# Layer two of a sixth batch in seven half-size products, scores in 64x32 tiles, and a new order of all pieces

## The chip, the cores and the metric

The kernel runs on one core of a Trainium2 chip. The metric is the device time of one execution in microseconds (us), the median of several runs. PE is TensorE (PEld its weight loads), DVE is VectorE, ACT is ScalarE, POOL is GpSimd, SP is SyncE, which here only issues DMAs.

## The reference

Eight batches, each with 8 heads of 512 tokens by 64 channels (`x`) and 32 states by 64 channels (`state`). Cross attention goes both ways, and the result, 544 rows by 512 channels for each batch, goes through a two-layer network:

```python
scores  = scale * x @ state.T;  a  = softmax(scores)     # per head, over 32 states
xread   = a @ state
scores2 = scale * state @ x.T;  a2 = softmax(scores2)    # per head, over 512 tokens
sread   = a2 @ x
X = concat([xread, sread], axis=2)                       # then heads side by side: (8*544, 512)
h = X @ w_in                                             # 512 -> 2048
g = s * relu(h)**2 + b
out = g @ w_out                                          # 2048 -> 512
```

## The kernel before

**An order written out by hand.** The whole kernel is a list of words, `ORDER`. Each word calls one small function (`pieces`), which issues its instructions; every engine executes its instructions in the order of the words. A word is a name and its arguments: `M.3.0.0` is batch 3, columns 0 to 511 of w_in; a last letter A, V or G names the engine (ACT, DVE, POOL). `idle.12` issues twelve matmuls on ones, whose result nobody uses (tile `dps`).

**Attention.** For a batch, `x` loads the tokens as half floats (`xh`), `xT` turns them in 32x32 blocks on DVE, and `T` computes the scores on PE: for each of two channel halves `e`, four head places `hp` and two head groups `g`, one matmul of a 32x32 tile, so 16 for a batch, with states from `stE`, which `pair` makes by a block transpose of the states `stn`. Group g writes half g of the tile T. `keep` copies scores to SBUF. Then, for the first softmax, U (transpose), mu (max), D (subtract), E1 (exp), z (sum and reciprocal), At (scale) and A (transpose). The second softmax is nm, nms, E2, a2; `aps` and `a2T` transpose it, `V` multiplies it with the tokens in another layout (`xn`), and `srd` keeps the result for the rows of all states, which go through the network at the end (`lsr`, `ssr`, `S_sr`, `P_sr`, `ev_sr`). In batch 0, x, xT, T and the first softmax come in two halves (a last argument 0 or 1), and part of its tokens come through `xf` and `castx`.

**Layer one.** Since xread = a @ state, the kernel first multiplies states and w_in: `M` is eight matmuls in 64x32 tiles (tile `mps`), and `Mc` copies the result to SBUF as half floats. Then `l.b.f` is two matmuls of 512 columns for one of 16 feature blocks (tile `hps`) and a relu on ACT; `s` squares two or four of them into the tile `g`. `lh` and `sh` are the same for half of batch 0's tokens.

**Layer two, direct.** `L.b.rr.q` is four matmuls of 512 columns; four of them make a token block of 128 rows, which `out` scales, shifts (on DVE) and stores. Sixteen L for a batch.

**Layer two, in seven products.** For batches 3 to 7 tokens, features and output channels are each split in two, and the eight half-size products become seven, with sums of halves: `S` makes sums of g on DVE or POOL (S1, S2, S4 in place, S3 in a tile of its own), `wsum` makes T1 to T4 from w_out once, `P.b.u` (u from 0 to 13) is eight steps of 256 columns times two row blocks, half of one product, `ev` takes a finished product out of PSUM on DVE, and `put` stores. The banks X, Y and W share two PSUM buffers with the direct products. A product that goes into X again waits until the one before has been evicted:

```python
PRODUCTS = [
    ("X", (0, 0), (0, 0)), ("Y", (0, 1), (1, 0)), ("X", (0, 0), "T2"), ("W", (1, 0), "T1"),
    ("X", None, "T3"), ("W", (0, 1), (1, 1)), ("X", (1, 1), "T4"),
]
```

The output tiles `osx_0` and `osx_1` exist once each, so that a batch's first eviction waits for the stores of the batch before.

**Queues.** POOL issues the loads of weights, tokens and states (`win`, `wout`, `x`, `xn`, `st`) in one queue with its own arithmetic; SP issues nearly all stores.

Of the kernel before, what the change touches and what calls it, by code (L numbers as in the profile page):

```python
# [10 lines left out]
FP32 = mybir.dt.float32  # L11
FP16 = mybir.dt.float16
# [66 lines left out]
def kernel(  # L79
# [12 lines left out]
    nc = tc.nc  # L92
    AF = mybir.ActivationFunctionType
    ALU = mybir.AluOpType
    AX = mybir.AxisListType

    B, H, S, D = x.shape
    Ns = state.shape[2]
    DM = H * D
    DF = moe_w_in.shape[1]  # L100
    P = 128
    NK = DM // P
    NKF = DF // P
    NG = H // 4
# [3 lines left out]
    NR = B * H * Ns // P  # L108
# [51 lines left out]
    stE = konst.tile([P, NR, Ns, 2], FP16, name="stE")  # L160
# [60 lines left out]
    nc.vector.memset(ones32, 1.0)  # L221
    xh_t[0] = xpool.tile([P, NG, NT, D], FP16, name="xh_0", tag="xh")
# [32 lines left out]
    def pair_states(i0, i1):  # L255
        nc.vector.transpose(
            stE[:, i0:i1].rearrange("p i n e -> p (i n e)").bitcast(FP32),
            stn[:, i0:i1].rearrange("p i d -> p (i d)").bitcast(FP32),
        )

# [33 lines left out]
    def at_T(b, own=1, p=None):  # L294

        at[b]["T", p] = T = two_banks(f"T_{b}_{p}", own=own)
        for e in range(2):
            for hp in range(4):
                for g in range(NG):
                    r = hp ^ g  # L300
                    mm(
                        part(T[Ns * hp : Ns * hp + Ns], p, g)[:, 0, :],
                        stE[32 * r : 32 * r + 32, NG * b + g, :, e],
                        part(at[b]["xT"][32 * r : 32 * r + 32, :, :, e], p, g)[:, 0, :],
                        start=(e == 0), stop=(e == 1),
                        tp=(32 * r, Ns * hp),
                    )
# [450 lines left out]
```

## Time and profile before

| | |
|---|---|
| time, median of 3 runs | 218.65 us (218.47 to 218.85) |
| the profiled execution | 218.68 us, span 216.8 us |
| granted PE clock, mean | 0.998 |
| busy: PE, DVE, ACT, POOL | 95%, 78%, 71%, 48% of the span |
| DMA | 103 GB/s on average, 153 to 205 GB/s in the first 32 us |

The page gives busy times by engine, the granted clock, and the chain of work that ended last. In the timeline a row is a group of instructions with its start, its time, the engine, the line and the tiles (out<-in), and in brackets the engine's idle time before it with what ended it. A row of windows is a stretch, its length, and the busy time of PE, PEld, DVE, ACT and POOL, each with its count, then the clock, the DMA share and GB/s. Matmuls overlap: the time of one in the trace is longer than the distance to the next.

### The profile page before, as it was taken

Reading aid. Unit: us, or ns where it says so; the run is one execution under the profiler, and the core shown is the slowest. Engines: PE = TensorE matmul, PEld = TensorE weight load, DVE = VectorE, ACT = ScalarE, POOL = GpSimd, SP = SyncE. Lnnn points to the kernel's source line nnn. Section 1 sums busy time; section 2 is a strip of 40 time slices with the busy share of each in tenths; the row PEclk is TensorE's granted clock in tenths of the full one; section 3 lists DMA queues with packets and bytes.
Section 4 is the critical chain, followed back from the end, with each engine's and each line's share of the span. In section 5 each row is a group of like instructions: output and inputs, shape, how many; then the busy total and the mean of one; then the engine's idle time right before and its main releaser. Section 6 shows DMA issues by size and latency. Waiting matters only on the chain.

```text
span 216.8 us, 4729 instructions
## 1 busy us (share of the span) xinstructions
PE 207.0 (95%) x1920; PEld 126.4 (58%) x1920; DVE 169.4 (78%) x236; ACT 154.7 (71%) x262; POOL 105.0 (48%) x102
## 2 busy tenths in 40 slices
PE   7668999999999999999999999999999999999992
PEld 2334444344444434545677666776667777888881
DVE  2699885989867879986998799979887964785571
ACT  4378987898858788899889899667668866444400
POOL 8529123494679930525254318836564334225330
PEclk9999999999999999999999999999999999999999
DMA  6999992759497262192908850718903600450055
GB/s 153 186 205 205 199 197 42 125 124 133 106 173 120 48 99 49 38 155 55 144 9 137 139 110 4 97 39 139 205 10 65 131 0 3 87 111 0 0 153 141
DMA packets 23657, 22.42 MB, mean 103 GB/s; under 512 B 4436, under 2 KB 17492, under 8 KB 23636
## 3 DMA queue, kind: packets, MB, share of 16 engines
q0 software_dynamic: 16848, 12.52, 40.8%
q1 hardware_dynamic: 5504, 8.66, 16.4%
q10 hardware_dynamic: 1284, 0.95, 1.6%
q8 instruction: 15, 0.25, 0.5%
q14 instruction: 6, 0.05, 0.1%
HBM read 25.72 MB, written 8.91 MB: 160 GB/s over the span
## 4 chain that ended last, share of the span: by engine, by line
PE 90%; ACT 5%; DMA 2%; DVE 0%; issue 0%; SPq 0%
PE hps L461 24%; PE ops L505 19%; PE opf_X L137 16%; PE opf_W L137 8%; PE mps L137 4%; PE opf_Y L137 4%; PE hps_sr L461 3%; PE vps L137 2%; DMA xf<-in_x_dram 2%; ACT M L152 2%; PE aps L137 2%; PE ops_sr_X L137 2%; PE T_None L137 2%; ACT rh L491 1%; PE dps L672 1%; PE hph L137 1%
## 5 line engine op out<-in xcount | busy, mean ns | idle before, releaser
L465 ACT ACTIVATE r<-hps 128x512 f16<-128x512 f32 x120 | 67.5, 602 | 27.8 <-PE hps L461 26.3
L461 PE MATMUL hps<-A,M 128*128 128x512 f16 x240 | 64.7, 380 | 0.0
L137 PEld LDWEIGHTS <-g 128*128 128x128 f16 x480 | 46.6, 98 | 11.4 <-issue 0.7
L505 PE MATMUL ops<-w_out,g 128*128 128x512 f16 x192 | 46.3, 379 | 0.0
L471 POOL TENSOR_TENSOR g<-r 128x1024 f16<-128x1024 f16 (+1 forms) x14 | 30.4, 2180 | 23.7 <-ACT r L465 23.7
L461 PEld LDWEIGHTS <-M 128*128 128x128 f16 x240 | 21.7, 98 | 22.7 <-issue 6.2
L505 PEld LDWEIGHTS <-g 128*128 128x128 f16 x192 | 18.7, 98 | 22.2 <-issue 0.4
L152 ACT CAST M<-mps 128x1024 f16<-128x1024 f32 x22 | 22.3, 1017 | 1.6 <-PE mps L137 1.5
L469 ACT ACTIVATE g<-r 128x1024 f16<-128x1024 f16 (+1 forms) x18 | 21.4, 1210 | 0.1
L192 POOL DMA_DIRECT2D xn<-in_x_dram x32 | 18.6, 592 | 5.6 <-PE vps L137 4.9
L346 POOL TENSOR_TENSOR At<-E,rz 128x1024 f16<-128x1024 f16 x5 | 9.8, 1964 | 22.0 <-ACT r L465 11.3
L137 PE MATMUL opf_X<-w_T,g 128*128 128x256 f16 x160 | 19.8, 272 | 0.0
L575 DVE TENSOR_TENSOR g<-g 128x1024 f16<-128x1024 f16 (+1 forms) x20 | 17.9, 908 | 1.1 <-POOL S L575 0.9
L575 POOL TENSOR_TENSOR g<-g 128x1024 f16<-128x1024 f16 x4 | 8.8, 2207 | 19.6 <-PE opf_X L137 12.4
L471 DVE TENSOR_TENSOR g<-r 128x1024 f16<-128x1024 f16 (+1 forms) x18 | 14.7, 836 | 1.6 <-ACT r L465 1.6
L152 DVE CAST M<-mps 128x1024 f16<-128x1024 f32 x10 | 12.1, 1213 | 3.5 <-PE mps L137 3.0
L604 DVE SCALAR_TENSOR_TENSOR osx<-opf_X,sb_bc,bias_bc 128x512 f32<-128x512 f32 x15 | 11.2, 746 | 4.0 <-PE opf_X L137 3.9
L292 DVE STREAM_TRANSPOSE xT<-xh 128x1024 f32<-128x1024 f32 (+2 forms) x12 | 10.4, 869 | 4.7 <-ACT xh L152 4.1
L325 POOL TENSOR_TENSOR Dm<-U,mu 128x1024 f32<-128x1024 f32 x3 | 5.7, 1913 | 15.0 <-DVE mu L321 15.0
L465 ACT ACTIVATE r_sr<-hps_sr 128x256 f16<-128x256 f32 x16 | 6.1, 382 | 7.9 <-PE hps_sr L461 7.2
L137 PE MATMUL mps<-w_in,stT 64*32 64x512 f16 x256 | 11.2, 383 | 0.3
L515 DVE SCALAR_TENSOR_TENSOR osb<-ops,sb_bc,bias_bc 128x512 f32<-128x512 f32 x12 | 8.8, 737 | 3.4 <-PE ops L505 3.4
(101 smaller groups left out, 324.3 us busy)
## 6 DMA issues: line engine op xcount, KB each, us to landing
out_dram<-osx SPq DMA_DIRECT2D x36, 128.0 KB, 2.4
xn<-in_x_dram POOLq DMA_DIRECT2D x32, 128.0 KB, 5.1
xh<-in_x_dram POOLq DMA_DIRECT2D x14, 256.0 KB, 5.1
w_in<-in_moe_w_in_dram POOLq DMA_DIRECT2D x8, 256.0 KB, 8.3
w_out<-in_moe_w_out_dram POOLq DMA_DIRECT2D x4, 512.0 KB, 11.2
out_dram<-osb SPq DMA_DIRECT2D x16, 128.0 KB, 2.6
out_dram<-osb SPq DMA_DIRECT2D x16, 64.0 KB, 4.4
xf<-in_x_dram SPq DMA_DIRECT2D x2, 256.0 KB, 3.7
```

The lines of the kernel that those rows point to most:

```text
L137: return nc.tensor.matmul(out, lhsT, rhs, start=start, stop=stop, tile_position=tp, is_transpose=is_transpose, skip_group_check=skip,)
L152: (engine.copy if engine is nc.scalar else engine.tensor_copy)(out, in_)
L192: nc.gpsimd.dma_start(out=xn_t[b][32 * jh : 32 * jh + 32].rearrange("t h c d -> t h (c d)"), in_=x[b].rearrange("h (t jh c) d -> jh t h (c ...
L292: nc.vector.transpose(part(out, p, g), part(in_, p, g))
L346: e.tensor_tensor(out, E1, over_n(rz), ALU.mult)
L461: nc.tensor.matmul(hps, lhsT, rhs, start=(i == 0), stop=(i == len(terms) - 1))
L465: nc.scalar.activation(R_t[tag, q][:, i], hps, AF.Relu)
L469: nc.scalar.activation(g, r, AF.Square)
L471: e.tensor_mul(g, r, r)
L505: nc.tensor.matmul(ops_t[tag, rr], G_t[tag][:, f, P * rr : P * rr + P], w_out_f(f), start=(f == 0), stop=(f == NKF - 1),)
L575: e.tensor_tensor(out, x, y, op)
L604: nc.vector.scalar_tensor_tensor(out, fast(b, name[0]), s_bc, out if plus else bias, ALU.mult, ALU.add)
```

## The change

1. Batch 2's layer two is done in seven products, as in batches 3 to 7: 16 words L and 4 words out go; 14 P, 8 half sums S, 7 ev and 4 put come (P 70 to 84, ev 35 to 42, put 20 to 24), and the sums of w_out are made earlier, eight half ones on DVE.
2. `T` uses 64x32 tiles, the size that `M` uses. Two states share the 64 rows of a tile, so the states are stored twice, `stZ[0]` and `stZ[1]`, each with the other's rows zero: `pair` transposes, then scales by a column of ones and zeros (`own`) twice. Heads are placed by `hp ^ 2 * g` instead of `hp ^ g`.
3. The words stand in a new order with other engines: squares on ACT, DVE, POOL from 18, 18, 14 to 11, 30, 9; M's casts on ACT and DVE from 22, 10 to 29, 3; V in six words instead of four; idle from 12, 12 and 5 to 7, 5 and 4. Only the beginning of the list is shown.

```diff
 ORDER = [
-    "x0.1 x0.0 castx.1.A xT.0.1.0 casts.A idle.12 pair.0.4 castx.0.A xT.0.0.0 T.0.1.0 U.0.0 turn.0.4.A "
-    "mu.0.0 D.0.V.0 E1.0.0 sb idle.12 keep.0.0 xT.0.1.1 win.0 M.1.0.0 M.0.0.1 x.1 z.0.0 xT.0.0.1 At.0.V.0 "
-    "A.0.0 win.1 wout.0 T.0.0.1 U.0.1 Mc.1.0.A mu.0.1 D.0.V.1 Mc.0.0.A lh.0.2.0 xT.1.1 lh.0.0.0 keep.0.1 "
-    "xT.1.0 idle.5 E1.0.1 win.2 M.0.1.0 T.1.1 sh.0.0.0.V Mc.0.1.A z.0.1 At.0.V.1 A.0.1 lh.0.6.0 lh.0.4.0 "
...
+    "casts.A pair.0.4 castx.1.A idle.7 xT.0.1.0 castx.0.A xT.0.0.0 x0.1 xT.0.1.1 x0.0 idle.5 turn.0.4.A "
+    "T.0.1.0 U.0.0 win.0 win.1 keep.0.0 x.1 win.2 wout.0 xT.0.0.1 T.0.0.1 mu.0.0 D.0.V.0 win.3 keep.0.1 "
+    "U.0.1 M.1.0.1 M.0.0.0 E1.0.0 Mc.1.0.A z.0.0 mu.0.1 D.0.V.1 At.0.V.0 A.0.0 wout.1 Mc.0.0.A E1.0.1 "
+    "idle.4 st z.0.1 At.0.V.1 M.0.1.1 Mc.0.1.A M.1.1.0 Mc.1.1.A xT.1.0 A.0.1 x.2 lh.0.2.0 sh.0.2.0.V "
+    "lh.0.0.0 sh.0.0.0.V lh.0.6.0 sh.0.6.0.V lh.0.2.1 xT.1.1 sh.0.2.1.V wout.2 sb lh.0.4.1 M.0.2.0 "
...
-    stE = konst.tile([P, NR, Ns, 2], FP16, name="stE")
+    stZ = [konst.tile([P, NR, Ns, 2], FP16, name=f"stZ_{k}") for k in range(2)]
+    own = konst.tile([P, 2], FP32, name="own")
...
+    nc.vector.memset(own, 0.0)
+    for r in range(4):
+        nc.vector.memset(own[Ns * r : Ns * r + Ns, r % 2 : r % 2 + 1], 1.0)
...
         nc.vector.transpose(
-            stE[:, i0:i1].rearrange("p i n e -> p (i n e)").bitcast(FP32),
+            stZ[0][:, i0:i1].rearrange("p i n e -> p (i n e)").bitcast(FP32),
             stn[:, i0:i1].rearrange("p i d -> p (i d)").bitcast(FP32),
         )
+        for k in (1, 0):
+            nc.vector.tensor_scalar(stZ[k][:, i0:i1], stZ[0][:, i0:i1], own[:, k : k + 1], None, ALU.mult)
...
-                    r = hp ^ g
+                    r = hp ^ 2 * g
+                    rows = slice(64 * (r // 2), 64 * (r // 2) + 64)
                     mm(
                         part(T[Ns * hp : Ns * hp + Ns], p, g)[:, 0, :],
-                        stE[32 * r : 32 * r + 32, NG * b + g, :, e],
-                        part(at[b]["xT"][32 * r : 32 * r + 32, :, :, e], p, g)[:, 0, :],
+                        stZ[r % 2][rows, NG * b + g, :, e],
+                        part(at[b]["xT"][rows, :, :, e], p, g)[:, 0, :],
                         start=(e == 0), stop=(e == 1),
-                        tp=(32 * r, Ns * hp),
+                        tp=(64 * (r // 2), Ns * hp),
                     )
```

The part of the new order that the middle of batch 4's seven products comes from:

```
... M.6.0.1 a2.6 s.4.12.4.V S.4.3.0.V S.4.3.1.V M.5.3.0 ev.3.X4
l.5.0 Mc.6.0.A put.2.1.0 put.2.1.1 put.3.0.0 l.5.6 P.4.2 P.4.3 x.7 S.4.1.2.V z.6 At.6.V l.5.3 P.4.0
S.4.2.0.G xT.7 Mc.5.3.A P.4.1 ev.4.X1 ev.4.Y l.5.4 l.5.1 aps.6 a2T.6.A S.4.2.1.V s.5.0.2.V l.5.9
P.4.4 P.4.5 l.5.5 T.7.1 M.6.2.0 put.3.0.1 keep.7 A.6 ev.4.X2 ...
```

More of the change, by code (lines that the diff above doesn't have):

```diff
@@ L410, in at_V @@
                 for g in range(NG):
-                    hp = k ^ g
+                    hp = k ^ 2 * g
                     for i in range(SCH):
@@ L430, in at_M @@
             for g in range(NG):
-                r = hp ^ g
+                r = hp ^ 2 * g
                 mm(
```

113 rows, old and new, of the table ORDER are left out of this document.

## The prediction

> **What bounds the kernel now.** I read the page's busy shares, the chain of waits, PE's own waits, then PE's timeline.
>
> ```profile
> PE 207.0 (95%) x1920; PEld 126.4 (58%) x1920; DVE 169.4 (78%) x236; ACT 154.7 (71%) x262; POOL 105.0 (48%) x102
> PE 90%; ACT 5%; DMA 2%; DVE 0%; issue 0%; SPq 0%
> ```
>
> PE is busy 95% of the span and is 90% of the chain that ends last. Its waits (us in total, times, longest) lie in the first 22 us:
>
> ```profile
> PE T L137 <- DVE xT L292: 1.3, 1, 1.3
> PE T L137 <- ACT M L152: 0.9, 1, 0.9
> PE hph L137 <- ACT M L152: 0.7, 2, 0.5
> PE hph L137 <- ACT rh L491: 0.3, 1, 0.3
> ```
>
> After that matmuls start one behind the other, so what counts is the distance from start to start, not the duration of one. PE's timeline (start, us, engine, line):
>
> ```profile
> 27.04 1.89 PE L505 MATMUL ops<-w_out,g 128*128 128x512 f16 x8
> 28.77 0.59 PE L461 MATMUL hps<-A,M 128*128 128x512 f16 x2
> ...
> 48.80 0.59 PE L461 MATMUL hps<-A,M 128*128 128x512 f16 x2
> 49.33 0.64 PE L137 MATMUL T_None<-xT,stE 32*32 32x512 f16 x16
> 49.90 0.41 PE L137 MATMUL mps<-w_in,stT 64*32 64x512 f16 x8
> 50.25 1.04 PE L461 MATMUL hps<-A,M 128*128 128x512 f16 x4
> ...
> 164.14 1.91 PE L137 MATMUL opf_X<-w_T,g 128*128 128x256 f16 x16
> 165.89 1.03 PE L461 MATMUL hps<-A,M 128*128 128x512 f16 x4
> ```
>
> Eight full matmuls take 28.77 - 27.04 = 1.73 us (0.216 each), sixteen half-size ones 165.89 - 164.14 = 1.75 us (0.109 each). Words of ORDER thus cost PE: L 0.863, P 0.873, l 0.432, lh 0.436. Added up so, the words behind L.0.1.1 (ended 28.77) come to 183.4 us; PE ended 212.49, so the remaining 0.3 us is all the waiting in 184 us.
>
> **Product form.** Batch 2 loses 16 L (16 x 0.863 = 13.81) and gains 14 P (14 x 0.873 = 12.22): **-1.60 us** on the path.
>
> **Tiles.** A T costs 0.57 (49.33 to 49.90) and the M behind it 0.35; two M in a row take 0.56 in all. I read this as 0.22 per eight matmuls, 0.12 at the end of each stretch of one tile size, and 0.10 on entering. Before there are 23 entries and 29 stretches, after 26 and 26, since T and M now share a size: 3 x 0.10 - 3 x 0.12 = about -0.1 us. Bounds: T as before (+0.3), or one entry fewer for each pair (-0.5).
>
> **V.** Six words instead of four; a pair costs 1.14 and an entry 0.10, so +0.2 us (up to +1.1 if a single V cost as much as a pair). Dense work: -1.60 - 0.1 + 0.2 = **-1.5 us**.
>
> **The start** I follow instruction by instruction from rows. The first T still waits for the second half of xf (cast at 5.63, transposed by 6.73), so it stays at 6.78: the five small memsets and two scalings in front of it end earlier. No row shows a scaling of this shape; the nearest (L388, 128x512) is 0.363, the memset of 128x512 0.485. I take 0.2 each for the first pair and 0.5 for the second (384 columns before, scaled as 768), with zero and twice that as ends. DVE now does U, mu and D of both halves before the first z chain ends, so A.0.0 ends near 13.8 (12.7 before); ACT casts four M before the first relu, which begins near 15.7 (13.99 before). On POOL nothing but DMA issues stands before sh.0.4.0, while in before w_in 3 was issued behind a square that waited for ACT to 14.67. Landings in before are some 2.45 us per weight load from 10.6 (w_in 0) to 23.8 (w_in 3); in the new order that puts w_in 1 at 13, w_in 2 at 18.0 (21.2 before), w_out 0 at 20.5 (17.9 before), w_out 1 at 25.5, w_out 2 near 32. With relus of 0.55 from 15.7 and these landings L.0.1.1 ends at 29.3, with 14.6 us of useful PE work done (14.2 at 28.77 before): **+0.1 us**. Bounds: -0.5 (relus start earlier) to +1.0 (a landing late). The fillers (29 dps before, 16 now) only fill gaps.
>
> **The rest.** ACT's work by rows goes from 174.2 to 176.1, POOL's from 106.0 to 87.4, DVE's from 178.8 to 191.4 (out 12 to 8, ev 35 to 42, S 26 to 41, s 18 to 30, Mc 10 to 3) plus 1.4 for the scalings. For these PE is the cover, where DVE keeps up:
>
> ```profile
> 100.00:150.00 50.00, 50.00 (x557) 35.06 (x556) 44.17 (x64) 41.94 (x70) 26.07 (x27) 1.00 0.56 90
> ```
>
> DVE is busy 44.2 of 50 us here (fifth column). In this stretch rows give 46.5 us of DVE words before and 50.5 after, so 48 of 50 us are to be expected. Following DVE's queue from ev.2.X4 to ev.4.W2, I find every result ready before PE needs it, but barely: S.4.2.1 0.1 us before P.4.5, ev.4.X1 0.5 before P.4.4; at P.2.7 S.2.1.1 comes 0.1 late. One wait is new: batch 3's ev.3.X1 writes the single osx_0 that batch 2 now uses, and z, At, xT and the sums of batches 3 to 6 queue behind it on DVE. Batch 2's last eviction into it ends near 92.7, its four stores (2.4 us to landing, some 0.5 us apart on SP) are out by 97, ev.3.X1 is due at 98.3; were it late, P.3.4 at 104.4 would be the first to feel it. Batch 2's stores stay eight of 128 KB. I allow 0.7 us of waits where before has 0.3: **+0.4 us**, bounds 0 and +2.5. The end is unchanged: seven small products, one eviction of 0.48 and a store.
>
> Sum: -1.5 + 0.1 + 0.4 = **-1.0 us**. The profiled execution took 218.68 (span 216.8), the median is 218.65; so **217.7 us**.
>
> **Rivals.**
>
> *DVE comes too late* (slower). Each product into bank X waits until the one before is evicted, and evictions stand in DVE's queue behind z, At, xT and sums. From S.3.2.0 to ev.4.Y thirty instructions hold about 24.5 us and run from 102.8 to 128.3 with 0.5 us to spare. If DVE needs over 2% more than my rows, P.4.4 waits; at 6% it is 1.5 us less the 0.5, and about 1 us again in the next 20 us, since PE has no slack to make it up. With -1.1 from the other terms: near **219.6**. For it: one-half sums take 0.69 to 0.78 us by shape, and 2.04 at 194.15, while POOL worked too. Against: POOL has 18.6 us less to do, and before holds 88% without a wait.
>
> *A slow PE clock in the start* (about no change). The granted clock reads 1.00 everywhere, yet the first fillers start 0.43 apart:
>
> ```profile
> 1.46 4.05 PE L672 MATMUL dps<-ones 128*128 128x512 f16 x12 [1.46 <-DVE ones L220]
> ...
> 8.19 2.76 PE L672 MATMUL dps<-ones 128*128 128x512 f16 x12
> ```
>
> The second twelve run at 0.22. In the changed kernel both first groups run out near 5.5, and until M at 10.7 PE has only two T, two transposes and the like, 1.3 us of work in 5.2. If it falls back to half speed there, four M, the four fillers and the first two lh take twice their 1.1, 0.9 and 0.9 us; part lies beside ACT's casts, so it costs 0.6 to 1.2, and the result is **218.6**. The Trainium skill, "TensorE: Matmul & The Clock Gate", Part 1, says that the array's clock halves after an idle window of about 3.4 us and returns after a busy one; the first twelve fillers agree, while a stretch as thin as this one is shown by no run here. By that rule the slow stretch would be likely, by the row at 8.19 (full speed after 2.7 thin us) not.
>
> *The wider tile is slower.* If products of two row positions into one half of T took turns, a T would go from 0.57 to about 1.0 and seven full and two half ones would cost +3.4: **221**. Against: in before four row positions write into each half, and T costs what M costs, where each half has one row position. The Trainium skill, "TensorEngine Tiling (Array Packing)", Gotcha 1, says that different row tiles cannot use one PSUM bank at once; the 0.57 against 0.56 speaks against a cost.
>
> *The start gains* (faster): w_in 2 lands 3 us sooner, and if relus keep pace L.0.1.1 ends at 28.6 and waits stay at 0.3: **216.5**.
>
> **How the numbers follow.** Chances: forecast 0.49, DVE late 0.24, slow clock 0.12, wider tile 0.04, start gains 0.11. A measurement here tells 0.2% (0.44 us). The forecast's own range is 216.7 to 218.5. Faster: most of the forecast (0.44), the start that gains and little of the clock: 0.58. Same: 0.05 of the forecast, 0.07 of the clock and some of DVE late: 0.15. Slower: the rest, 0.27. The range leaves out the wider tile and the worst of DVE: 216.1 to 219.9.
>
> **What would show it.** Right: L.0.1.1 ends near 29.3, from there to PE's end some 182.2 us, P of batch 2 at 0.873, a T in front of an M at 0.44 to 0.46, DVE at 95% in the 100 to 150 window. Wrong: PE waiting for osx, g or S on DVE in the middle; lh or M at twice their distance before 20 us; T near 1 us.

## The result and the profile after

| | before | after |
|---|---|---|
| median of 20 runs each, same chip | 218.76 us (218.24 to 219.44) | 218.13 us (217.52 to 218.81) |
| ratio after to before, 95% interval | | 0.9967 [0.9957, 0.9978] |
| profiled execution (span) | 218.68 us (216.8) | 217.52 us (215.7) |
| L.0.1.1 ends | 28.77 | 29.13 |
| last product starts | 211.62 | 210.59 |
| between the two | 182.85 | 181.46 |

The kernel is faster by 0.72 us by the ratio (0.0033 of 218.76; interval 0.48 to 0.94); the two medians differ by 0.63. The forecast was 1.0 us and 217.7; the measured median lies inside its own range. The profiled execution of the changed kernel is the fastest of its twenty, so its distance from before (1.16 us) is more than the usual one. The last row of the table is used throughout: "the body" is the time from L.0.1.1's end to the start of the last product. The two orders do not put the same work ahead of it: in the changed kernel PE has done two `l` and the four transposes of turn.4.12 more by then and one `lh` less, 0.65 us by rows.

The page, busy shares and the chain that ended last:

```profile
PE 205.8 (95%) x1955; PEld 130.0 (60%) x1955; DVE 179.6 (83%) x277; ACT 158.0 (73%) x260; POOL 86.9 (40%) x94
PE 91%; DMA 3%; ACT 2%; POOL 1%; DVE 1%; issue 0%; POOLq 0%
```

PE is still the chain. DVE went from 78% to 83% of the span, POOL from 48% to 40%. PE's waits (us in total, times, longest):

```profile
PE T L141 <- DVE xT L302: 1.8, 2, 1.2
PE dps L683 <- DVE ones L225: 1.5, 1, 1.5
PE mps L141 <- DMA w_in<-in_moe_w_in_dram: 1.3, 2, 0.9
PE hph L141 <- ACT rh L502: 0.7, 1, 0.7
PE mps L141 <- DVE M L156: 0.4, 1, 0.4
```

All of these lie before 26 us; behind that the profile shows no wait of PE at all. PE's timeline (start, us) at the two places that the prediction named:

```profile
58.99 0.65 PE L141 MATMUL T_None<-xT,stZ 64*32 64x512 f16 x16
59.46 0.40 PE L141 MATMUL mps<-w_in,stT 64*32 64x512 f16 x8
59.79 0.61 PE L472 MATMUL hps<-A,M 128*128 128x512 f16 x2
...
82.43 1.91 PE L141 MATMUL opf_Y<-w_out,g 128*128 128x256 f16 x16
84.17 1.04 PE L141 MATMUL opf_X<-w_T,g 128*128 128x256 f16 x8
85.05 0.59 PE L472 MATMUL hps<-A,M 128*128 128x512 f16 x2
```

T in front of M takes 59.46 - 58.99 = 0.47 (before 0.57), and T and M together 0.80 where before they took 0.92. Two P of batch 2 take 84.17 - 82.43 = 1.74 and one takes 0.88, as P of the other batches did before (one P is eight matmuls: four steps of 256 columns times two row blocks). The stage from 100 to 150 us (PE, PEld, DVE, ACT, POOL busy, then PE's clock):

```profile
100.00:150.00 50.00, 50.00 (x574) 35.42 (x575) 47.57 (x73) 43.33 (x71) 20.11 (x25) 1.00 0.53 91
```

DVE is busy 47.6 of 50 us (48 forecast, 44.2 before), and PE is full.

### The profile page after: what moved, and what is told of

It reads as the page before. It is cut to its first block, busy times and chain, and to the rows that moved or that the text cites. A ratio compares the mean times of both kernels' runs of the same rounds, so it can differ in the third digit from the quotient of the medians.

```text
span 215.7 us, 4829 instructions
## 1 busy us (share of the span) xinstructions
PE 205.8 (95%) x1955; PEld 130.0 (60%) x1955; DVE 179.6 (83%) x277; ACT 158.0 (73%) x260; POOL 86.9 (40%) x94
## 4 chain that ended last, share of the span: by engine, by line
PE 91%; DMA 3%; ACT 2%; POOL 1%; DVE 1%; issue 0%; POOLq 0%
PE hps L472 25%; PE opf_X L141 20%; PE ops L516 13%; PE opf_W L141 10%; PE opf_Y L141 5%; PE mps L141 5%; DMA w_in<-in_moe_w_in_dram 3%; PE hps_sr L472 3%; PE vps L141 2%; PE aps L141 2%; PE ops_sr_X L141 2%; PE T_None L141 2%; ACT M L156 1%; PE hph L141 1%; PE ops_sr_W L141 1%; PE dps L683 1%
## 5 line engine op out<-in xcount | busy, mean ns | idle before, releaser
L482 POOL TENSOR_TENSOR g<-r 128x1024 f16<-128x1024 f16 (+1 forms) x9 | 21.3, 2372 | 27.0 <-ACT r L476 22.8
L156 ACT CAST M<-mps 128x1024 f16<-128x1024 f32 x29 | 29.2, 1013 | 2.3 <-PE mps L141 1.9
L516 PE MATMUL ops<-w_out,g 128*128 128x512 f16 x128 | 30.7, 379 | 0.0
L482 DVE TENSOR_TENSOR g<-r 128x1024 f16<-128x1024 f16 (+1 forms) x30 | 22.1, 754 | 1.6 <-ACT r L476 1.6
L586 POOL TENSOR_TENSOR g<-g 128x1024 f16<-128x1024 f16 (+1 forms) x3 | 8.3, 2768 | 15.4 <-PE opf_X L141 8.1
L141 PE MATMUL opf_W<-w_out,g 128*128 128x256 f16 x96 | 12.4, 273 | 0.0
L141 PE MATMUL opf_W<-w_T,g 128*128 128x256 f16 x96 | 12.3, 273 | 0.0
L141 PE MATMUL opf_X<-w_out,g 128*128 128x256 f16 x96 | 12.1, 273 | 0.0
L141 PE MATMUL opf_X<-w_T,S 128*128 128x256 f16 x96 | 11.8, 273 | 0.0
L141 PE MATMUL opf_Y<-w_out,g 128*128 128x256 f16 x96 | 11.8, 273 | 0.0
```

Of the source, the lines that this page charges most:

```text
L141: return nc.tensor.matmul(out, lhsT, rhs, start=start, stop=stop, tile_position=tp, is_transpose=is_transpose, skip_group_check=skip,)
L156: (engine.copy if engine is nc.scalar else engine.tensor_copy)(out, in_)
L482: e.tensor_mul(g, r, r)
L516: nc.tensor.matmul(ops_t[tag, rr], G_t[tag][:, f, P * rr : P * rr + P], w_out_f(f), start=(f == 0), stop=(f == NKF - 1),)
L586: e.tensor_tensor(out, x, y, op)
```

## The experiments

Each kernel was timed beside the kernel before on the same chip; ratios are to that, with 95% intervals. The changed kernel's own is 0.9967.

### Product form: direct, direct2, pe8

**direct** puts batch 2 back to the direct form:

```
-P.2.0 ... P.2.1 ... P.2.13            (fourteen P, with S.2.*, ev.2.*, put.2.*)
+L.2.0.0 ... L.2.0.3 out.2.0 ... L.2.3.2 L.2.3.3 out.2.3   (sixteen L, at the places of the P)
```

> The changed kernel with batch 2's layer two direct: sixteen L and four out in the places of its fourteen P, no S, ev or put for batch 2. My theory: PE pays the product form's 1.60 us back and nothing else changes: 218.04 + 1.6 = 219.6, ratio to before 1.004; DVE has some 8 us less to do and that is worth nothing. Rival, DVE's load is what costs in the changed kernel: part of the 1.6 comes back and the ratio is 0.998 to 1.001.

Measured: 223.74 us, ratio 1.0244 [1.022, 1.0268], some 6 us above the changed kernel. Compared start by start with the changed kernel, PE is 0.45 later at L.0.1.1 and 2.07 later at the `l` that starts at 96.15 there (l.4.2): 1.62 us have come on. Fourteen L stand there against twelve P, 1.60 by the rows, and the last two of each cost the same, so this is the product form, neither more nor less. What follows is another thing. PE at 104 us, and DVE at the same time:

```profile
104.93 1.03 PE L466 MATMUL hps<-A,M 128*128 128x512 f16 x4
107.84 0.65 PE L135 MATMUL T_None<-xT,stZ 64*32 64x512 f16 x16 [1.88 <-DVE xT L296]
```

```profile
105.13 0.75 DVE L520 SCALAR_TENSOR_TENSOR osb<-ops,sb_bc,bias_bc 128x512 f32<-128x512 f32 x1 [3.98 <-PE ops L510]
105.80 0.74 DVE L609 SCALAR_TENSOR_TENSOR osx<-opf_X,sb_bc,bias_bc 128x512 f32<-128x512 f32 x1
106.46 1.24 DVE L296 STREAM_TRANSPOSE xT<-xh 128x1024 f32<-128x1024 f32 x1
```

The eviction out.2.3 stood at the head of DVE's queue for 3.98 us, waiting for L.2.3.3, and xT.6 stood behind it, so that T.6.1 came 1.9 us late. A second wait (0.9 us at 156, P.5.4) makes up most of the rest, and it is of another kind: ev.5.X1, which P.5.4 needs, writes osx_0, and batch 4's last store out of osx_0 landed at 155.07 by the trace, 5.2 us after its issue, so that the eviction started at 155.25. In the changed kernel that store landed at 148.30, 2.4 us after its issue, and the same eviction started at 149.38. By these times it is the wait for the single osx_0 that the prediction named, at another batch; why the store took longer is open. So the surplus came from the places that I gave to the words and from that store, not from PE's work.

**direct2** moves the last two L and their eviction forward:

```
-L.2.3.0 L.2.3.1 l.4.2 ... l.4.5 L.2.3.2 L.2.3.3 out.2.3
+L.2.3.0 L.2.3.1 L.2.3.2 L.2.3.3 out.2.3 l.4.2 ... l.4.5
```

> The changed kernel with the sixteen L and four out of batch 2 in place of its fourteen P, sums and evictions, as in the run before it (direct), but with L.2.3.2, L.2.3.3 and out.2.3 right behind L.2.3.1, so that the last eviction of batch 2 no longer holds up ev.3.X1 and xT.6 in DVE's queue. Product form is worth 1.6 us (direct's trace shows PE 1.62 later at the end of batch 2, and the other 3 us as waits behind that eviction): 1.6 to 2.2 us more than the changed kernel, ratio to before 1.004 to 1.007, and no wait of PE at T.6.1. Rival, that products in the direct form cost more than their rows or leave DVE too late in any place: 3 us or more over the changed kernel, ratio above 1.010.

Measured: 223.41 us, 1.0197 [1.0162, 1.0233]; the rival's figure, not mine. The wait did not go, it changed its owner:

```profile
105.87 1.08 PE L466 MATMUL hps<-A,M 128*128 128x512 f16 x4 [0.85 <-ACT r L470]
107.27 0.65 PE L135 MATMUL T_None<-xT,stZ 64*32 64x512 f16 x16 [0.31 <-ACT M L150]
```

With five L in one piece (95.5 to 99.9) ACT got no `l` to work on for 2.7 us and then had to catch up; and DVE's out.2.3 still waited 2.7 us. A clean time of the product form alone was not to be had by moving words by hand. It stands on the trace of direct (1.62 us up to 96), and on **pe8**, which asks whether PE's work counts there in full:

```
-P.2.11
+P.2.11 idle.8
```

> The changed kernel with eight more full matmuls of ones on PE (1.73 us by the distance of 0.216 each, into a tile that nothing reads) right behind P.2.11. Theory behind the product term, that PE's work counts in full there: +1.5 to +1.75 us against the changed kernel, ratio to before 1.004 to 1.005. Rival, that DVE at 95% sets the pace behind it and hides part of PE's work: +1.0 us or less, ratio 1.001.

Measured: 220.78 us, 1.0112 [1.0088, 1.0135], 2.65 us above the changed kernel: more than expected. One line tells why:

```profile
94.35 1.89 PE L678 MATMUL dps<-ones 128*128 128x512 f16 x8 [0.84 <-DVE osx L610]
```

The eight matmuls needed a bank of their own and had to wait until DVE had evicted one; 1.73 us of work and 1.0 us in front of it. PE is 2.73 us later at the next `l` (3.19 against 0.46 at L.0.1.1) and still 3.19 later at the last product, 118 us further on. That is the useful part: what PE loses there, of whatever kind, is not made up by as much as 0.05 us.

### Tiles: small_tile, tile_alone, tile_late

**small_tile** has the new ORDER and products with the old 32x32 tiles and one copy of the states:

```
-r = hp ^ 2 * g ; stZ[r % 2][rows, ...], tp=(64 * (r // 2), Ns * hp)
+r = hp ^ g     ; stE[32 * r : 32 * r + 32, ...], tp=(32 * r, Ns * hp)
```

> The changed kernel's order and its six batches in seven products, but the scores in 32x32 tiles from one copy of the states, as in before. My theory: four dense places where T and M stand side by side cost 0.12 us more each, and one in the start is hidden: +0.5 us against the changed kernel, and nothing for the scalings that go (they are covered): 0.999 of before. Rival, the tile brings nothing: 0.9967 as the changed kernel. Rival, the scalings cost something in the start: below 0.996.

Measured: 218.52 us, 0.9990 [0.9978, 1.0001]: 0.5 us above the changed kernel, as expected. Its body is 181.92, 0.46 longer, in four steps of 0.11 or 0.12, each where T and M stand side by side:

```profile
59.31 0.64 PE L136 MATMUL T_None<-xT,stE 32*32 32x512 f16 x16
59.88 0.41 PE L136 MATMUL mps<-w_in,stT 64*32 64x512 f16 x8
```

T takes 0.57 here and 0.47 with the wide tile. Without an M behind it, both take the same (in the changed kernel 33.80 to 34.38, 0.58). So the width of the tile costs nothing and the change of size costs 0.11 or 0.12.

**tile_alone** has the new tiles with the old ORDER:

```
-ORDER = [ ...of the changed kernel... ]
+ORDER = [ ...of the kernel before... ]
```

> The order of before, with only the 64x32 score tiles and the states stored twice. My theory: a T beside an M no longer pays 0.12 us for the change of tile size, at six places: -0.7 us; but the two scalings of the second pair (0.87 us on DVE) stand right in front of xT.2, for which PE already waited 0.3 us at T.2.1, so +0.9 there: about +0.2 us against before in all (0.999 to 1.002). Rival, all the gain is from the tile: 0.997. Rival, the wider tile is slower in itself: over 1.01, with T near 1 us in the trace.

Measured: 219.97 us, 1.0058 [1.0039, 1.0076], 1.3 us above before: about 1 us more than expected. Compared start by start with before, PE gains 0.11 at each of three places where T and M stand side by side, but loses at two others:

```profile
39.08 0.65 PE L134 MATMUL T_None<-xT,stZ 64*32 64x512 f16 x16 [0.52 <-DVE xT L295]
...
51.75 1.04 PE L465 MATMUL hps<-A,M 128*128 128x512 f16 x4 [0.51 <-DVE A L360]
```

```profile
37.00 0.87 DVE L262 TENSOR_SCALAR stZ<-stZ,own 128x768 f16<-128x768 f16 x2
37.79 1.24 DVE L295 STREAM_TRANSPOSE xT<-xh 128x1024 f32<-128x1024 f32 x1
```

The scalings of pair.4.16, 0.79 us from 37.00 to 37.79, stand right in front of xT.2 in DVE's queue. I had expected the first wait (0.59 later there, 0.9 expected) and not the second (0.56 at the `l` behind A.2, which the expectations call A.2's squares). DVE was not still behind from the scalings: before xT.3 it stood idle for 1.08 us, waiting for a load. x.3 is issued by POOL behind a small copy (`ahead`) that reads xT.2:

```profile
39.09 0.28 POOL L178 COPY ahead<-xT 1x2 f16<-1x2 f16 x1 [2.25 <-DVE xT L295]
45.73 1.25 DVE L295 STREAM_TRANSPOSE xT<-xh 128x1024 f32<-128x1024 f32 x1 [1.08 <-DMA xh<-in_x_dram]
```

In before the copy starts at 37.82 and xT.3 at 43.96. With xT.2 late the load went out 1.27 us later, and xT.3, and A.2 behind it in DVE's queue (49.21 before, 50.98 here), came 1.77 later. In the new ORDER the same scalings stand behind xT.2 and T.2.1 does not wait.

**tile_late** pairs fewer states ahead of xT.2:

```
-pair.4.16 xT.2 ... T.2.1
+pair.4.8  xT.2 ... T.2.1 pair.8.16
```

> The kernel before with the wide tiles (as tile_alone), but only the states of batches 2 and 3 are paired and scaled ahead of xT.2, and the rest behind T.2.1: pair.4.8 and pair.8.16 in place of pair.4.16. In tile_alone PE was 0.59 us later at T.2.1 and 0.56 more at A.2's squares, both behind 1.74 us of scalings in DVE's queue. Theory, that the tiles themselves gain (0.11 at each of three places where M follows T) and only the place of the scalings costs: T.2.1's loss falls to 0.2 at most, A.2's stays or halves; ratio 1.000 to 1.004, against 1.0058 of tile_alone. Rival, that the wide tile itself costs: no change, 1.006.

(The 1.74 us of scalings in this text should read 0.79: the row's 0.87 is for both.)

Measured: 219.54 us, 1.0042 [1.0026, 1.0057], at the edge between theory and rival, so the time alone decides nothing. In the trace T.2.1 and the M behind it lose 0.13 where they lost 0.65 in tile_alone, the `l` behind A.2 loses nothing, and a new wait has come:

```profile
43.11 0.63 PE L134 MATMUL mps<-w_in,stT 64*32 64x512 f16 x16 [1.11 <-ACT Ts L317]
```

pair.8.16 now stands in front of U.2; the M at 42.19 of before needs the banks of T.2, which come free behind U.2 and the copy, and falls back by 1.2 us against the words ahead of it. Everywhere else the body only gains (0.11 or so at the same three T). So in all three kernels the tile itself gains, and the scalings cost what stands behind them in DVE's queue, loads that wait for it included. No run here has the wide tile in the old order without such a wait.

### DVE's slack: dve1, dve3, dve3_late

```
-xT.7 Mc.5.3.A P.4.1 ev.4.X1 ev.4.Y
+xT.7 dve.1 Mc.5.3.A P.4.1 ev.4.X1 ev.4.Y        (dve3: dve.3)
...
+    def more_dve(n):
+        for _ in range(n):
+            nc.vector.memset(spare, 0.0)
```

> The changed kernel with one more memset of 128x512 on DVE (0.485 us by the row of the other one, into a tile that nothing reads), right behind xT.7. The trace of the changed kernel has ev.4.X1 done 0.7 us before P.4.4 and S.4.2.1 done 0.2 us before P.4.5. Theory, that DVE still has this slack: P.4.5 waits 0.3 us at most, total 0 to +0.3 us, ratio 0.9967 to 0.998. Rival, that DVE at 95% already sets the pace of PE there: +0.5 us or more, ratio 0.999.

> As dve1, with three memsets (1.45 us). Theory: P.4.4 and P.4.5 wait 0.75 to 1.25 us, PE has no slack behind them to make it up, so the end comes 0.8 to 1.3 us later, ratio 1.000 to 1.003; more than 1.5 us if evictions behind it are late too. Rival, that DVE catches up before PE needs it: no change, ratio 0.9967.

Measured: **dve1** 218.04 us, 0.9957 [0.9942, 0.9973]; **dve3** 218.91 us, 1.0000 [0.9986, 1.0014]. A memset took less than I had assumed: counted from the start of xT.7, three moved S.4.2.1 by 1.03 us and one by 0.20. In dve1 PE loses 0.05 there, in dve3 0.90; two of dve3's rows:

```profile
129.95 1.03 PE L136 MATMUL opf_X<-w_T,g 128*128 128x256 f16 x8 [0.21 <-DVE osx L610]
131.34 1.05 PE L136 MATMUL opf_X<-w_T,g 128*128 128x256 f16 x8 [0.36 <-DVE g L581]
```

P.4.4 waits for ev.4.X1 (osx) and P.4.5 for S.4.2.1 (g), the two that the prediction named. Of 1.03 us on DVE, 0.90 reached PE, and the median rose by 0.87 over dve1. The slack at P.4.5 is thus 0.13 to 0.15 us.

**dve3_late** puts the same three elsewhere:

```
-ev.5.W2
+dve.3 ev.5.W2
```

> The changed kernel with the three memsets of dve3 (1.45 us on DVE), but right ahead of ev.5.W2, where DVE waits 2.26 us for PE. Theory, that what counts is the slack at the place and not DVE's share of the span: no change, ratio 0.9957 to 0.9975. Rival, that DVE's work counts wherever it stands: +0.9 us as in dve3, ratio 1.000.

Measured: 218.08 us, 0.9967 [0.9955, 0.9979]: no change. DVE's wait there in the changed kernel, and in this one:

```profile
163.62 0.75 DVE L615 SCALAR_TENSOR_TENSOR osx<-opf_W,sb_bc,osx 128x512 f32<-128x512 f32 x1 [2.26 <-PE opf_W L141]
```

```profile
164.02 0.75 DVE L610 SCALAR_TENSOR_TENSOR osx<-opf_W,sb_bc,osx 128x512 f32<-128x512 f32 x1 [1.21 <-PE opf_W L136]
```

The memsets filled a wait that was there anyway. Equal work on DVE costs 0.9 us at 128 and nothing at 162.

### The start: warm

```
-U.0.0 ... T.0.0.1
+U.0.0 idle.4 ... T.0.0.1 idle.7
```

> The changed kernel with eleven more filler matmuls: four behind the first U, seven behind the second T of batch 0, so that PE is not thin between 7 and 10.3 us. The granted clock of 0.50 to 0.83 between 11 and 15 us should read 1.00. Theory one, the slow stretch is hidden beside ACT's casts and w_in's landings: ratio as the changed kernel, 0.996 to 0.9975, and L.0.1.1 ends at 29.1 or 28.9. Theory two, the slow clock costs its 0.6 to 1.2 us on the path: 0.991 to 0.994, and L.0.1.1 ends near 28.3.

Measured: 218.16 us (217.86 to 218.32), 0.9965 [0.9948, 0.9982], the same as the changed kernel. The stretch from 12 to 13 us (the clock is the number behind the five engines' busy times), first the changed kernel, then warm:

```profile
12.00:13.00 1.00, 1.00 (x10) 0.24 (x16) 1.00 (x2) 1.00 (x2) 0.43 (x1) 0.50 1.13 207
```

```profile
12.00:13.00 1.00, 0.33 (x9) 0.04 (x9) 1.00 (x2) 1.00 (x2) 0.56 (x1) 1.00 1.17 214
```

The clock did fall to a half in the changed kernel, and the fillers kept it up; the time did not move. In warm's profile L.0.1.1 even ends at 29.81, because w_in landed later (M.0.2 waits until 18.86, in the changed kernel it runs at 18.01), and its body is 181.45 against 181.46. From M.0.0.0 at 10.3 us up to that landing PE's words start within 0.4 us of the changed kernel's, now earlier, now later (16.78 against 16.62 at lh.0.2.1), so the full clock had brought nothing by then either. The changed kernel's own twenty runs say the same: the eight with a mean granted clock of 0.980 to 0.984, so with more slow time, took 217.98 us on average, the twelve with 0.988 to 0.992 took 218.14. So the start's end is set by casts, relus and landings, and a slow PE there is hidden.

### Single small words: paired, paired_fill

The changed kernel has its bias sums in two groups and M.2.0 alone. **paired** joins them:

```
-cps.0 cps.1 l.1.2 ... M.2.0.1 Mc.2.0.A ... T.2.1 l.1.0 ... cps.2 cps.3
+l.1.2 ... T.2.1 M.2.0.0 l.1.0 Mc.2.0.A ... cps.0 cps.1 cps.2 cps.3
```

> The changed kernel with cps.0 to cps.3 in one group (after: two groups of two) and M.2.0.0 right behind T.2.1 (after: alone between squares). By rows of the changed kernel: two groups of cps take 0.55 each and an entry of 0.10 each, against 0.97 and one entry in before: -0.2 us; M.2.0 alone takes 0.34 and an entry 0.10, behind T 0.22 and no entry: -0.2 us. Expected -0.3 to -0.4 us against the changed kernel, ratio to before 0.995. Rival, that the wider words only move a wait (bias or Mc.2.0 late for L.0.0.3 or L.0.2.0): no change, 0.9967.

Measured: 219.02 us, 1.0005 [0.9991, 1.0018], 0.9 us slower than the changed kernel where I expected 0.3 to 0.4 faster. Two of PE's waits are new:

```profile
PE hps L467 <- ACT r L471: 0.4, 2, 0.2
...
PE cps L136 <- ACT M L151: 0.3, 1, 0.3
```

With the words gone, ACT's relus set the pace from 29 to 34 us. The cps group and M that I took away had stood beside them: by rows 1.1 us of PE's work left that stretch, and it became 0.23 shorter. Where the larger group went it added its whole length and a wait for a pair of banks that M.2.0 still held. **paired_fill** puts 0.65 us of other work into the empty place:

```
-sh.0.6.1.G l.1.2
+sh.0.6.1.G fill.3 l.1.2
...
+    def fill(n):
+        t = two_banks("fill")[:, 0, :]
+        for _ in range(n):
+            mm(t, ones16[:, :P], ones16)
```

> The kernel paired with three full matmuls of ones (0.65 us, into a tile that nothing reads) where the changed kernel has cps.0 and cps.1, that is behind the lh and ahead of l.1.2. In paired, PE waits 0.25, 0.19 and 0.29 us for ACT in this stretch, and its end comes 0.8 us later. Theory, that ACT's relus set the pace there, so that the first cps group cost nothing where it stood: +0 to +0.25 us against paired, ratio 1.000 to 1.002. Rival, that PE's words there count in full and something else made paired slow: +0.65 us, ratio 1.0035.

Measured: 219.17 us, 1.0019 [1.0005, 1.0033]. Its body is 182.46 against 182.23 of paired: of 0.65 us of PE work 0.23 counted. The theory holds.

No kernel here is faster than the changed one beyond the noise; dve1, dve3_late and warm equal it.

## Why the prediction was right

**The sum, with luck in it.** The body is the steadiest number of this study: 181.46 in the changed kernel, 181.51 in dve1, 181.44 in dve3_late, 181.45 in warm, against 182.85 before. So the body gives -1.39 us. The start is what differs between executions: with the new start L.0.1.1 ended between 29.13 and 29.69 in ten profiles (the changed kernel, small_tile, direct, direct2, the three dve, the two paired, pe8), 29.43 on average; with the old order at 28.77, 29.11 and 28.38 (the last two with the wide tile), 28.75 on average. That is +0.68, and -1.39 + 0.68 = -0.71 beside the measured -0.72; three old starts that lie 0.7 apart do not carry the second decimal, so an agreement this close is chance. The prediction had 29.3 and 182.2 us from there to PE's end (182.33 measured): it was 0.13 too hopeful in each, which is its error of -1.0 against -0.72. But the parts of the body were not right one by one. Word by word, from start to start in both traces:

| part of the body, us | forecast | measured |
|---|---|---|
| product form | -1.60 | -1.59 |
| work moved ahead of L.0.1.1 | -0.4 | -0.65 |
| changes of tile size, V included | +0.1 | +0.8 |
| waits | +0.4 | +0.06 |
| sum | -1.5 | -1.39 |

The second and fourth were forecast 0.6 us too dear and the third 0.7 too cheap; that they nearly cancel is luck. (The -0.4 is the prediction's 14.2 against 14.6 us of work done.)

**Product form, -1.60.** Right: -1.59 by the two traces' own rows, and 1.62 in direct's trace.

**Tiles and V, -0.1 and +0.2.** The price of one change was right, and the count was the step that failed. One stretch of smaller tiles between full ones costs about 0.23 in the changed kernel:

```profile
92.88 1.03 PE L472 MATMUL hps<-A,M 128*128 128x512 f16 x4
93.84 0.62 PE L141 MATMUL mps<-w_in,stT 64*32 64x512 f16 x16
94.40 1.92 PE L141 MATMUL opf_X<-w_T,S 128*128 128x256 f16 x16
96.15 1.03 PE L472 MATMUL hps<-A,M 128*128 128x512 f16 x4
```

The two `l` take 0.96 for 0.86, the two M 0.56 for 0.43. The prediction counted T and M over the whole order, 23 entries and 29 stretches against 26 and 26. Two of the three stretches that it saved stand ahead of L.0.1.1, where PE is not what the time waits for. In the body PE goes from full tiles to smaller ones 20 times before and 25 times after (the bias sums in two groups, which the prediction left out, are one of the five), and from one smaller size straight to another 6 times before and 3 after: 5 x 0.23 - 3 x 0.115 = +0.8. What the wide tile saves is in this sum: between the forecast and its bound for T as before lay 0.4, and small_tile measures 0.46.

**Waits, +0.4.** The profile shows none behind 26 us, and the words bear it out: where two words have neighbours of the same tile sizes they take the same time in both kernels, and what exceeds this adds up to 0.03 us in the body before and 0.09 after. So the 0.3 of waiting that the prediction put into before was work priced too low, and the 0.7 that it allowed after did not come; the changes of tile size filled its place. The wait of 0.1 at P.2.7 is not there (P.2.7 starts at 86.78, right behind its forerunner).

**The start.** Landings came as predicted: w_in 2 at 17.85 (18.0 forecast, 21.20 before), w_out 0 at 20.40 (20.5). A.0.0 ended at 13.76, the first relu began at 15.34. The scalings took 0.26 each in the first pair (5.11 to 5.63 for two) and 0.40 in the second (32.60 to 33.40), for 0.2 and 0.5. With 0.65 us more of PE's work done at L.0.1.1's end and 0.68 us more time, the start as such gave and cost nothing (+0.1 forecast); the rival that the start gains (L.0.1.1 at 28.6) was met in no profile, though w_in 2 came 3.4 us sooner.

**DVE too late** (the rival that I gave 0.24). It did not happen, by about 0.14 us: dve3 shows it happening. DVE was at 47.6 of 50 us with every result in time, and 1.03 us more at one place took the gain away. The prediction's list of slacks was the right tool: it had 0.1 at P.4.5, where 1.03 - 0.90 = 0.13 was found, and 0.5 at P.4.4, where ev.4.X1 ended at 128.30 and the product started at 129.01. The new wait for osx_0 did not occur in the changed kernel, but it was nearer than forecast: batch 2's stores were out at 99.4 (97 forecast), and ev.3.X1 started at 100.11, behind D.5, which ended then. In direct a wait of this kind came at batch 5.

**Slow clock** (0.12). The condition came true and the price did not: half speed from 11.3 to 14.7 us, with the first lh at 0.83 (13.82 to 14.65) instead of 0.44, one of the signs that the prediction gave for being wrong. Yet L.0.1.1 ended at 29.13 for 29.3, and warm shows no gain without it. I had priced the slow matmuls as if PE were what the start waits for. The cases must be multiplied: the chance of the condition by the chance that its cost lies on the path.

**Wider tile slower** (0.04). Refuted by T's 0.58 against 0.57. The Trainium skill, "TensorEngine Tiling (Array Packing)", Gotcha 1, forbids different row tiles in one PSUM bank at once; no cost of it shows here, for two row positions or for four.

## What to carry to other kernels

Where PE is full, price a change by start-to-start distances of whole words and by what it does to the number of changes of tile size, and then follow the queue of the next busiest engine word by word: its share of busy time says little (95% cost nothing, and one more microsecond cost 0.9 at one place and nothing at another). Count the changes in the stretch where PE is full, not in the whole order. An instruction that waits at the head of a queue, or work put ahead of others in it, delays all behind it, and a load that is issued behind one of these comes late too: direct, tile_alone and tile_late each lost over 1 us in that way. And before a small word is taken out to save its time, look whether it stands in a stretch that another engine paces.

## What was not expected of the hardware

In all ten profiles with the new start PE's granted clock was 0.50 for one stretch, of 3.4 us in seven of them and 6.8 in small_tile, direct and paired, beginning anywhere from 8.2 to 11.5 us. In the changed kernel PE had been thin before, but not idle throughout: its rows add up to 1.8 us in the 3.4 us ahead of the drop at 11.3 (T 0.42, M 0.39 and 0.56, fillers 0.44). The Trainium skill, "TensorE: Matmul & The Clock Gate", Part 1, speaks of windows of about 3.4 us that run freely and of a slow clock after an idle one; the length and the shifting beginning agree. Here a window that was only thin was followed by the slow clock, and with warm's eleven fillers in it no slow stretch came. The longer stretch did not end the start later (29.33, 29.58 and 29.26, against 29.13 to 29.69 with the shorter).

A memset of 128x512 in half precision has a row of 0.48 in the start of before, and in dve3 the trace shows three of them as 128x256 of 32 bits, 0.27 each and 0.39 from start to start. The doses of the DVE experiments were smaller than their expectations say: 1.03 us for 1.45, and 0.20 for 0.485.
